# Where the seventh up group's third-block sums are made: last up group or first down unit

## The chip, the cores and the metric

The kernel runs on one core of a Trainium2 chip. The metric is the device time of one launch in microseconds (us), the median of three runs. The engines named below are PE (TensorE, the matrix multiplier; PEld is its weight load), DVE (VectorE), ACT (ScalarE), POOL (GpSimd) and SP (SyncE, which issues DMAs).

## The reference, cut to what matters

An attention with a cluster mask is followed by a two-layer feed-forward with a squared ReLU.

```python
q, k, v: (4, 8, 768, 64); centroids: (8, 16, 64)
mask = argmax(q_n . c_n) == argmax(k_n . c_n)
attn = softmax(where(mask, q k^T / 8, -1e9));  attn_out = attn v
x = attn_out.transpose(0, 2, 1, 3).reshape(3072, 512)
out = max(x @ w_in, 0) ** 2 @ w_out        # w_in 512 x 2048, w_out 2048 x 512
```

Only the second part is touched here. It is worked off in four sequences of 768 tokens each; the code numbers them n = 0 to 3.

## The kernel before, in words

Everything is float32. Matrix products are made by Strassen-like schemes: seven products in place of eight, for the price of sums and differences that DVE (and POOL, for `w_in`) makes. The result of the first layer, `g`, holds 16 blocks of 128 hidden rows by 2 halves of 384 tokens. A half is cut again into three blocks of 128 tokens: the first two are `TWO`, the third is `THIRD`.

**The up stage** (`up`, n = 1 to 3) runs over eight groups i = 0 to 7. A group makes four results, c11, c12, c21, c22: hidden rows i and 8+i for both token halves. PE makes products into PSUM banks, DVE adds a bank to a result (`add`, `sub`), ACT squares it (`square`, two instructions, L769 and L770; the last result of group 7 is squared by DVE, L773). Between these, DVE makes sums of finished groups for the next stage: `first_level` for the blocks `TWO`, `third_sums` for the block `THIRD`. In the last group the order on DVE is: product 6 added, `first_level(6)`, product 2 added to c11, `third_sums(6)`, product 7 added, then `behind_seven`, which is the first call of `parts`.

**`third_sums(g, n, f)`** makes four DVE instructions of 128 x 128 into a staging tile `third` (two buffers, shared with the output tiles), and its returned function stores that tile to DRAM, `g_far[n]`, with one DMA of 256 KB (L1105). For all f but the last it first calls `store_third`, which sends two more blocks of `g` there (L1092, and L1094 where n is even).

**The down stage** (`Down.run`) runs over units u, seven where n = 2 and fourteen where n = 1 or 3. A unit makes seven times eight 128 x 128 matmuls: with the sums in `s` (tile `l2`, shown as `l`), with the blocks of `g`, `home` or `extra`, and with four derived right factors that lie in `slot(0)` to `slot(3)`. In order: block times y00; block times y10; `s[:, 1]` times slot 1; a difference times slot 2; `s[:, 0]` times slot 0; a block times slot 3; and last a block from which DVE has subtracted `s[:, 1]` in place. `parts` makes the sums of the next unit. `combine` adds the banks up.

Where n is odd, units of the third blocks of two sequences (n-1 and n) are mixed in. Their left factors come back from `g_far` by `load_left(j)`, four DMAs of 256 KB or two where j is 1 or 4: into `g` for j = 4, into the tile `extra` for j = 1 and 5. The units there start (own, 1), (own, 4), (third, 4), (third, 1), (own, 5), (third, 5).

All loads and stores concerned are issued by SP in program order, each wait holding what is behind it. `load_right(k)`, called when the next unit needs other right factors, issues four DMAs of 256 KB from `w_far` into slots 1, 2, 0, 3, each when PE is through with the slot. In unit 0 of an odd sequence SP's order is: `load_right(4)`, `load_left(4)`, `load_left(1)`, the store of the last `third`, `load_left(5)`; the third of the four loads of `load_left(5)` reads what that store wrote. In unit 2 comes `load_right(1)`, for unit 3.

The order on every engine is written out by hand (`manual_schedule`), so the program order of the code is that of the engine's queue.

Of the kernel before, what the change touches and what calls it, by code (L numbers as in the profile page):

```python
# [25 lines left out]
def kernel(  # L26
# [521 lines left out]
    H2, F2, M2 = KT // 2, FT // 2, DM // 2  # L548
# [17 lines left out]
    def w_sums(i, odd=0):  # L566
        lo, hi = slice(i * P, (i + 1) * P), slice((F2 + i) * P, (F2 + i + 1) * P)
        a = [[w_in[:, H2 * g2 : H2 * (g2 + 1), cols] for g2 in range(2)] for cols in (lo, hi)]
        w_s = sp.tile([P, 4, H2, P], F32, name="w_s", tag=f"s{(i + odd) % 2 + 1}")
        s1, s2, s3, s4 = (w_s[:, j] for j in range(4))  # L570
        nc.gpsimd.tensor_tensor(out=s1, in0=a[1][0], in1=a[1][1], op=ALU.add)  # L571
        sub(s2, s1, a[0][0], nc.gpsimd)
        sub(s3, a[0][0], a[1][0], nc.gpsimd)
        sub(s4, a[0][1], s2, nc.gpsimd)
        return a, s1, s2, s3, s4
# [150 lines left out]
    def bank_tile(width):  # L726
        return banks.tile([P, width], F32, name="bank", tag="bank")
# [162 lines left out]
    def up(b, g, n, x, behind_seven):  # L890
        flat = g.rearrange("p f h n -> p (f h n)")
        odd = n == B - 1
        w_next = w_sums(0, odd)
        lefts, rights, done = {}, {}, []
        for i in range(F2):
            w, w_next = w_next, w_sums(i + 1, odd) if i + 1 < F2 else None
            ((c11, c12), (c21, c22)), product = group(i, g, w, x)
            ends, late = i >= F2 - 2, i % 2

            def result(j):  # L900
                bank = bank_tile(TB)
                product(j, bank)
                return bank

            def add(j, *results):
                bank = result(j)
                for out, to in results:
                    plus(out, bank, to)

            def levels_1():  # L910
                if done:
                    first_level(g, done[0])

            def levels_2():
                if done:
                    third_sums(g, n, done.pop(0))()

            def two():
                add(2, (c11, c11))
                square(c11)  # L920
                levels_2()

            if i < 2:
                nc.scalar.copy(out=c11, in_=result(1))
            elif not late:
                next(unit_1)
                if ends:
                    load_right(1)
            if not (late or ends):
                lefts[4] = second_lefts(4, i)  # L930
            add(6, (c12, c11))
            levels_1()
            if i == 1:
                rights[1] = second_rights(1, x[0][0][0])
            if not late or ends:
                two()
            if i == 0:
                rights[4] = second_rights(4, x[4])
            add(7, (c21, c12))
            if i == F2 - 1:  # L940
                behind_seven()
            elif ends:
                levels_1()
            r = spare_tile.rearrange("p i n -> p (i n)")
            if late and not ends:
                unit_4 = second(lefts.pop(4), rights[4], r, 0, TB)
                next(unit_4)
            add(5, (c22, c21), (c12, c12))
            square(c22)
            if i == F2 - 2:  # L950
                levels_2()
            if ends:
                sub(c21, c21, result(4))
            elif late:
                next(unit_4)
                unit_1 = second(
                    second_lefts(1, i + 1), rights[1], flat, 2 * TB * (i + 1), 2 * TB
                )
                next(unit_1)
                both = g[:, F2 + i - 1 : F2 + i + 1, 0]  # L960
                sub(both, both, r.rearrange("p (i n) -> p i n", i=2))
                for k in range(2):
                    square(both[:, k])
                two()
            add(3, (c12, c12))
            if ends:
                square(c21)
            (square if i < F2 - 1 else square_by_dve)(c12)
            done.extend([i] if ends else [i - 1, i] if late else [])
        xT.pop(b)  # L970
# [14 lines left out]
    def plus(out, one, two):  # L985
        nc.vector.tensor_tensor(out=out, in0=one, in1=two, op=ALU.add)  # L986
# [104 lines left out]
    def store_third(g, n, f):  # L1091
        nc.sync.dma_start(g_far[n][f, :, 1:3], g[:, F2 + f, :, THIRD])  # L1092
        if n % 2 == 0:
            nc.sync.dma_start(g_far[n][f, :, 0], g[:, f, 0, THIRD])  # L1094

    def third_sums(g, n, f):
        if f < F2 - 1:
            store_third(g, n, f)
        a = block_of(g, f, THIRD)
        third = outp.tile([P, DM], F32, name="third", tag="osb").rearrange("p (j n) -> p j n", j=4)  # L1100
        plus(third[:, 0], a[1][0], a[1][1])
        sub(third[:, 1], third[:, 0], a[0][0])
        sub(third[:, 2], a[0][0], a[1][0])
        sub(third[:, 3], a[0][1], third[:, 1])
        return lambda: nc.sync.dma_start(g_far[n][f, :, 3:7], third)  # L1105
# [12 lines left out]
    class Down:  # L1118
# [119 lines left out]
        def store(self, queue=nc.scalar):  # L1238
            for of, to in self.stores:
                for i in range(2):  # L1240
                    self.store_block(of, to, i, queue)
            self.stores = []

        def run(self):
            first_level(self.g, F2 - 1)
            store_third(self.g, self.n, F2 - 1)
            waiting = None
            for u, (of, j) in enumerate(self.units):
                x, s = self.ahead
                y = quarters(right(j))  # L1250
                copied = spare_tile[:, 4 + u % 2]
                one, two = (
                    bank_tile(4 * P).rearrange("p (i n) -> p i n", i=4) for _ in range(2)
                )

                ends = self.n == B - 1 and u + 1 == len(self.units)
                five = bank_tile(P) if ends else two[:, 3]
                last = bank_tile(P) if ends else None
                times(one[:, 0], x[0][0], y[0][0])
                nc.scalar.copy(out=copied, in_=one[:, 0])  # L1260
                self.store()
                times(two[:, 0], x[0][1], y[1][0])
                times(two[:, 1], s[:, 1], slot(1))
                times(two[:, 2], x[1][0], slot(2))
                times(five, s[:, 0], slot(0))
                times(one[:, 2], x[1][1], slot(3))
                if waiting:
                    next(waiting)
                sub(x[0][1], x[0][1], s[:, 1])
                times(last if ends else one[:, 1], x[0][1], y[1][1])  # L1270
                if u + 1 < len(self.units):
                    if (k := self.units[u + 1][1]) != j:
                        load_right(k)
                    if of and j in LATER:
                        self.load_left(LATER[j])
                    if self.units[u - 1] == (0, 5):
                        sub(self.s1, self.a[0][1], self.s2)
                    self.parts()
                if u == 0:
                    store = third_sums(self.g, self.n, F2 - 1)  # L1280
                    self.find_results()
                    if self.n % 2:
                        self.load_left(4)
                        self.load_left(1)
                    store()
                    if self.n % 2:
                        self.load_left(5)
                if waiting:
                    next(waiting, None)
                waiting = self.combine(of, j, one, two, five, copied, last)  # L1290
                to_end = len(self.units) - 1 - u
                for kk in LOADS[self.n % 2].get(u, ()):
                    load_x(self.n + 1, kk)
                if to_end == 2 - self.n % 2:
                    sum_x(self.n + 1, 1)
                elif to_end == 0:
                    sum_x(self.n + 1, 2)
            if self.n == B - 1:
                self.store(nc.sync)
            list(waiting)  # L1300
            sum_x(self.n + 1, 1)
            self.store()
# [298 lines left out]
```

## Time and profile before

| what | us |
|---|---|
| median of three runs (882.5 to 882.65) | 882.58 |
| the profiled execution's own time | 882.29 |
| its span, first to last instruction | 880.5 |
| PE busy / DVE busy / ACT busy | 871.7 / 753.9 / 385.9 |
| up stage to down stage, n = 1, 2, 3: first matmul of the down stage starts at | 512.48, 671.48, 786.54 |

The profile is of one execution; its times are microseconds from the span's start. PE's matmuls overlap one another, so a busy PE is read from the spacing of their starts: eight matmuls of the down stage start every 0.89 us when nothing holds them (514.27, 515.16, 516.06, 516.95). The granted clock is 1.0 in the whole execution. What lies around the span is 882.29 - 880.5 = 1.79 us.

### The profile page before, as it was taken

How to read it: one execution, taken by the hardware profiler on the slowest of the kernel's cores; microseconds unless marked ns; L12 is line 12 of the kernel's file. 1: busy time of each engine (PE TensorE's matmuls, PEld its weight loads, DVE VectorE, ACT ScalarE, POOL GpSimd, SP SyncE). 2: the span in 40 equal slices, each digit the busy share in tenths (PEclk: the TensorE clock that was granted, in tenths of full speed). 3: DMA queues.
4: the chain of work that ended last, by engine and by line, in shares of the span. 5: the costliest groups of instructions: out<-in, count | busy, mean ns of one | idle time of the engine just before them, and what ended most of it. 6: DMA issues, size and time to landing. Idle time of an engine off the chain costs nothing.

```text
span 880.5 us, 14989 instructions
## 1 busy us (share of the span) xinstructions
PE 871.7 (99%) x5487; PEld 600.3 (68%) x5487; DVE 753.9 (86%) x1359; ACT 385.9 (44%) x621; POOL 181.2 (21%) x240
## 2 busy tenths in 40 slices
PE   9999999999999999999999999999999999999997
PEld 6454444444444455568876689997767987769997
DVE  6798888888888999999859986797899898997786
ACT  5877667777765657750034420002443005440000
POOL 0000010000010236740055300005550064500000
PEclk9999999999999999999999999999999999999999
DMA  7887787766764335226701256681024730138563
GB/s 252 160 195 202 222 265 176 201 188 193 214 179 101 87 137 168 90 96 227 274 31 37 101 168 189 172 275 37 31 89 142 241 122 25 36 120 256 156 202 121
DMA packets 166402, 136.05 MB, mean 155 GB/s; under 512 B 58826, under 2 KB 140082, under 8 KB 166066
## 3 DMA queue, kind: packets, MB, share of 16 engines
q1 hardware_dynamic: 149938, 119.92, 46.6%
q10 hardware_dynamic: 16384, 15.11, 5.5%
q8 instruction: 45, 0.74, 0.3%
q14 instruction: 35, 0.29, 0.1%
HBM read 82.10 MB, written 41.89 MB: 141 GB/s over the span
## 4 chain that ended last, share of the span: by engine, by line
PE 76%; DVE 18%; ACT 2%; issue 2%; DMA 2%; DVEq 0%; ACTq 0%; SPq 0%
PE bank L1109 22%; PE bank L793 14%; PE sc L441 13%; PE av_a L475 9%; DVE g L986 7%; PE bank L1001 6%; PE av_b L475 4%; PE sc L450 3%; DVE third L551 2%; DVE g L551 2%; DVE spare L986 2%; DVE home L551 2%; PE sc L329 1%; DVE home L986 1%; PE sc L494 1%
## 5 line engine op out<-in xcount | busy, mean ns | idle before, releaser
L457 ACT ACTIVATE ex<-sc 128x1024 f32<-128x1024 f32 x144 | 144.2, 1025 | 38.1 <-PE sc L441 31.9
L441 PE MATMUL sc<-qkT 64*128 64x512 f32 (+1 forms) x768 | 151.0, 484 | 0.0
L986 DVE TENSOR_TENSOR g<-bank,g 128x384 f32<-128x384 f32 (+3 forms) x205 | 102.2, 514 | 19.8 <-PE bank L793 11.8
L769 ACT ACTIVATE g<-g 128x384 f32<-128x384 f32 x122 | 63.0, 516 | 98.2 <-DVE g L986 78.0
L441 PEld LDWEIGHTS sc<-qkT 64*128 64x128 f32 x768 | 67.2, 188 | 40.9 <-issue 29.7
L793 PE MATMUL bank<-xT,w_s 128*128 128x384 f32 x256 | 93.1, 486 | 0.0
L793 PE MATMUL bank<-x_t,w_s 128*128 128x384 f32 x256 | 93.0, 486 | 0.0
L1260 ACT COPY spare<-bank 128x128 f32<-128x128 f32 x35 | 9.2, 264 | 185.9 <-PE bank L1109 167.9
L475 PE MATMUL av_a<-ex,v_raw 128*64 128x512 f32 x384 | 85.9, 597 | 0.0
L460 DVE TENSOR_TENSOR total<-total,ex 128x1024 f32<-128x1024 f32 x64 | 78.7, 1229 | 6.5
L161 POOL TENSOR_TENSOR w_in<-w_in,w_raw 128x512 int32<-128x512 int32 x16 | 21.4, 1337 | 294.9 <-DVE w_in L153 294.9
L571 POOL TENSOR_TENSOR w_s<-w_in 128x256 f32<-128x256 f32 x32 | 25.3, 790 | 249.8 <-PE bank L1109 145.9
L1109 PE MATMUL bank<-home,l 128*128 128x128 f32 x560 | 74.1, 275 | 0.0
L793 PEld LDWEIGHTS bank<-xT,w_s 128*128 128x128 f32 x256 | 48.6, 190 | 34.2 <-issue 0.5
L1109 PEld LDWEIGHTS bank<-home,l 128*128 128x128 f32 x560 | 68.1, 192 | 0.1
L793 PEld LDWEIGHTS bank<-x_t,w_s 128*128 128x128 f32 x256 | 48.2, 190 | 29.1
L793 PE MATMUL bank<-xT,w_in 128*128 128x384 f32 x184 | 67.1, 487 | 0.0
L770 ACT ACTIVATE g<-g 128x384 f32<-128x384 f32 x122 | 63.8, 523 | 3.9
L475 PEld LDWEIGHTS av_a<-ex,v_raw 128*64 128x64 f32 x384 | 26.1, 137 | 51.0 <-issue 50.0
L450 PE MATMUL sc<-rows 64*128 64x512 bf16 (+1 forms) x360 | 60.4, 324 | 0.0
L793 PEld LDWEIGHTS bank<-xT,w_in 128*128 128x128 f32 x184 | 34.4, 190 | 21.7 <-DVE g L551 0.6
L1109 PE MATMUL bank<-home,g 128*128 128x128 f32 x352 | 46.5, 275 | 0.0
(222 smaller groups left out, 1559.9 us busy)
## 6 DMA issues: line engine op xcount, KB each, us to landing
home<-w_far SPq DMA_DIRECT2D x92, 256.0 KB
words<-flat SPq DMA_DIRECT2D x26, 384.0 KB
w_raw<-in_moe_w_in_dram SPq DMA_DIRECT2D x16, 512.0 KB
w_raw<-in_moe_w_out_dram SPq DMA_DIRECT2D x16, 512.0 KB
w_far<-home SPq DMA_DIRECT2D x28, 256.0 KB
g<-g_far SPq DMA_DIRECT2D x28, 256.0 KB
v_raw<-in_v_dram SPq DMA_DIRECT2D x16, 384.0 KB
g_far<-third SPq DMA_DIRECT2D x24, 256.0 KB
```

Of the source, the lines that this page charges most:

```text
L441: nc.tensor.matmul(sc[i][:, e, cols], lhsT=qkT[pair][rows, NCH + c], rhs=qkT[pair][rows, n.start // P : n.stop // P], start=first, stop=no ...
L450: nc.tensor.matmul(sc[i][:, e, cols], lhsT=ohT[pair][rows, 1, c * P : (c + 1) * P], rhs=ohT[pair][rows, 0, columns(i)], start=first, stop= ...
L457: nc.scalar.activation(out=ex[i], in_=sc.pop(i), func=ACT.Exp, scale=SCALE)
L460: eng.tensor_tensor(out=out, in0=a, in1=b, op=ALU.add)
L475: nc.tensor.matmul(bank[D * e : D * (e + 1), 0 : n.stop - n.start], lhsT=raw_v[pair][:, e, c], rhs=ex[i][:, e, cols], start=c == 0, stop=c ...
L551: return eng.tensor_tensor(out=out, in0=a, in1=b, op=ALU.subtract)
L769: nc.scalar.activation(out=to, in_=to, func=ACT.Relu)
L770: nc.scalar.square(to, to)
L793: nc.tensor.matmul(bank, lhsT=operands[j][0][:, kk], rhs=operands[j][1][:, kk], start=(kk == 0), stop=(kk == H2 - 1),)
L986: nc.vector.tensor_tensor(out=out, in0=one, in1=two, op=ALU.add)
L1001: nc.tensor.matmul(bank, lhsT=left[j][:, f], rhs=right(j)[:, f], start=(f == 0), stop=(f == F2 - 1),)
L1109: nc.tensor.matmul(bank, lhsT=left[:, f], rhs=rhs[:, f], start=(f == 0), stop=(f == F4 - 1))
```

## The change

In the last up group (i = 7) `third_sums(6)` is no longer called. In the down stage `store_third(6)` is called at the start, ahead of `store_third(7)`, and `third_sums(6)` just ahead of `third_sums(7)`, behind the first unit's `parts`. Both tiles are stored at the place where the last one was stored, behind `load_left(1)` in the odd sequences. This is so in each of n = 1, 2 and 3; n = 0 has other code.

```diff
             def levels_2():
-                if done:
+                if done and i < F2 - 1:
                     third_sums(g, n, done.pop(0))()
...
     def third_sums(g, n, f):
-        if f < F2 - 1:
+        if f < F2 - 2:
             store_third(g, n, f)
...
             first_level(self.g, F2 - 1)
-            store_third(self.g, self.n, F2 - 1)
+            for f in (F2 - 2, F2 - 1):
+                store_third(self.g, self.n, f)
...
                 if u == 0:
-                    store = third_sums(self.g, self.n, F2 - 1)
+                    stores = [third_sums(self.g, self.n, f) for f in (F2 - 2, F2 - 1)]
                     self.find_results()
                     if self.n % 2:
                         self.load_left(4)
                         self.load_left(1)
-                    store()
+                    for store in stores:
+                        store()
                     if self.n % 2:
                         self.load_left(5)
```

No instruction is added or taken away: in each of the three sequences four DVE instructions, one store of a `third` tile and the place of the `store_third` DMAs in the queue move.

## Prediction

> **What bounds the kernel now.** I read the page's busy shares first, then the groups for PE's idle time, then the timeline of PE, DVE, ACT and SP about the change from up to down stage.
>
> ```profile
> PE 871.7 (99%) x5487; PEld 600.3 (68%) x5487; DVE 753.9 (86%) x1359; ACT 385.9 (44%) x621; POOL 181.2 (21%) x240
> ...
> L1109 PE MATMUL bank<-w_out,g 128*128 128x128 f32 x240 | 30.0, 276 | 1.8 <-DVE g L551 1.8
> ```
>
> PE has hardly any idle time, but 1.8 us of it lies in the down stage, behind a DVE instruction of L551 (`sub`). PE's timeline for n = 1 shows where:
>
> ```profile
> 516.95 1.06 PE L1109 MATMUL bank<-home,g 128*128 128x128 f32 x8
> 518.62 1.16 PE L1109 MATMUL bank<-w_out,g 128*128 128x128 f32 x8 [0.61 <-DVE g L551]
> 519.61 1.95 PE L1109 MATMUL bank<-w_t,g 128*128 128x128 f32 x16
> ```
>
> These are unit 0's last eight matmuls. At a spacing of 0.89 they would start at 517.84; they start at 518.62 (0.78 late), and the next at 519.61, 0.99 later in place of 0.89 (0.10 more, the first weight load not overlapped). The stall costs 0.88; n = 2 and 3 show the same gap (0.62 and 0.61). So all that DVE can win here is 3 x 0.88 = 2.64. DVE is back to back from 509.4 to the awaited `sub` (517.87 to 518.56). The moved work lies in that chain, in group 7:
>
> ```profile
> 510.12 0.55 DVE L986 TENSOR_TENSOR g<-bank,g 128x384 f32<-128x384 f32 x1
> 510.58 0.28 DVE L986 TENSOR_TENSOR third<-g 128x128 f32<-128x128 f32 x1
> ...
> 511.26 0.52 ACT L770 ACTIVATE g<-g 128x384 f32<-128x384 f32 x1
> 511.31 0.29 DVE L551 TENSOR_TENSOR third<-g,third 128x128 f32<-128x128 f32 x1
> 511.51 0.55 DVE L986 TENSOR_TENSOR g<-bank,g 128x384 f32<-128x384 f32 x1
> 511.98 0.68 DVE L986 TENSOR_TENSOR l<-g 128x512 f32<-128x512 f32 x1
> ```
>
> The reader is to see that c11 of group 7 is added at 510.12, squared by ACT until 511.78, and that `l<-g`, the first sum of `parts` for unit 0, comes at 511.98. That sum reads all eight c11 blocks, so it needs this square.
>
> [...] The record of `l<-g` has one, which waits for ACT: it runs at 511.814, 0.036 behind the end of the square; at n = 2 and 3 it stands 0.037 behind too. [...] here a lone `third` store lands after 2.0 and in a full queue after 4.3 to 4.6, which I use.
>
> **The change part by part.** *Taken out of group 7:* four DVE instructions. By their starts (510.58 to 511.51) they hold DVE 0.93. But `l<-g` cannot follow by 0.93: the wait for ACT ends at 511.81, and where such a wait ends last DVE starts 0.066 later, at 511.88 in place of 511.98. The gain is 0.10 for each n; the other 0.83 becomes DVE idle time. c11's own square does not come earlier, since the add before it waits for `first_level(6)`, which waits for ACT. The rest of the chain to the `sub` moves up by 0.10 (its ACT square, c22's, moves with it). Bounds: 0 (the wait already decides) and 0.88 (it doesn't exist). I take 0.10: total -0.30.
>
> *Added behind unit 0's `parts`:* the same 0.93, so all DVE work from there on is 0.93 - 0.10 = 0.83 later than before. Behind it wait `combine` of unit 0 and unit 1's `sub`, which ended at 523.14 and is needed by about 524.8; at 523.97 it is in time (n = 2: 682.96 for 683.8; n = 3: 798.37 for 798.9, the tightest). DVE had 1.20 (n = 1), 1.34 and 0.75 of idle time one unit later and catches up there. POOL and ACT have nothing queued here that matters. Cost 0. Were that cover gone, up to 0.83 for each n.
>
> *SP and the transfers, n = 3:*
>
> ```profile
> 785.68 0.32 SPq L1105 DMA_DIRECT2D g_far<-third  x1
> ...
> 793.24 2.98 SPq L1146 DMA_DIRECT2D g<-g_far  x2
> 796.28 1.05 SPq L1146 DMA_DIRECT2D extra<-g_far  x2
> 797.37 0.50 SPq L1105 DMA_DIRECT2D g_far<-third  x1
> 797.91 4.97 SPq L1146 DMA_DIRECT2D extra<-g_far  x4
> 802.98 0.45 SPq L1068 DMA_DIRECT2D home<-w_far  x1
> ```
>
> The store at 785.68 is the one that moves, out of an idle queue and to just ahead of 797.37, where the queue is full. The DMA completion marks in the trace give the landings: `load_left(4)` at 798.32 and 799.60, `load_left(1)` at 800.47 and 801.29, the store at 801.96, then 802.80 and 803.62. Only when the store had landed did SP issue the third load of `load_left(5)` (801.97), and only behind that could it issue `load_right(1)` (802.98). `store_third(6)` costs nothing: its data are ready by 508 (n = 1), and SP is idle until 516.57.
>
> What is late next is `load_right(1)`. (a) One store more in a full queue: 0.67, the distance of the store's landing from the one before it. (b) The second load of `load_left(4)` overwrites what `third_sums(7)` reads, so it is issued 0.83 later (795.85 to 796.68). It was bound half by the queue, half by its own latency (3.74; 3.07 for a like load into a nearly empty queue), so it lands between 0 and 0.83 later; I take 0.6. Together d = 1.27 (0.67 to 1.5). All that follows lands later by d. The slots are used by PE in these rows:
>
> ```profile
> 807.96 1.06 PE L1109 MATMUL bank<-home,l 128*128 128x128 f32 x8
> 808.86 1.06 PE L1109 MATMUL bank<-home,g 128*128 128x128 f32 x8
> 809.75 1.06 PE L1109 MATMUL bank<-home,l 128*128 128x128 f32 x8
> 810.64 1.06 PE L1109 MATMUL bank<-home,g 128*128 128x128 f32 x8
> ```
>
> They landed at 807.20, 808.19, 809.39, 810.04: 0.76, 0.67, 0.36, 0.60 ahead. The smallest lead decides: PE is late by d - 0.36 + 0.05 (restart) + 0.10 (weight load, as in the stall above) = 1.06 against before. *n = 1:* leads 1.19, 1.44, 1.68, 1.85; d - 1.19 + 0.15 = 0.23 late. *n = 2:* no left factors are loaded, `load_right(5)` comes behind the stores, with a lead of 0.70 at the least; one store more (0.67) fits: the gain of 0.10 stays.
>
> **Sum:** +0.23 - 0.10 + 1.06 = +1.19. On the profiled execution's 882.29 (span 880.5 and 1.79 around it) that is 883.48; the median stands 0.29 above that execution, so I forecast 883.8, no change that can be told: about 0.2%, 1.77 us, is what a measurement of this kernel can tell from none.
>
> **The rivals.** *Transfers hidden:* the extra store is absorbed because later loads were spaced by PE's release of the slots (804.58 and 805.48 were), not by the queue. Against it: their latency is 4.8 and 4.6, a lone one's 2.8. Then only -0.30 stays: 882.3. *Slower beyond doubt:* the same loads stall PE in both odd sequences. n = 1 differs from n = 3 only by a faster last megabyte (531.66 to 534.74, against 805.89 to 810.04). The two stalls exceed 1.77 together, with n = 2's 0.10 taken off, from d = 1.57 on ((d - 0.21) + (d - 1.04) - 0.10); at d = 1.8 they make 2.25: 884.8. For it: (b) may be the whole 0.83 and hold up every load behind it. Against: that takes 0.07 more than (a) and (b) at their ends. *The change does what it says:* the ACT wait is no limit, the stall goes, 2.64 less: 879.9. Against it are three event records at the same 0.036 behind ACT.
>
> **How the numbers follow.** Forecast (a stall at `load_right(1)`, d 0.7 to 1.57): 0.60. Transfers hidden: 0.13. Slower: 0.23. Stall gone: 0.04. Faster by over 0.2% is the last, 0.04; slower the third, 0.23; within 0.2% the other two, 0.73. The range leaves out the fast rival and the slow one's far end: from 882.1, under the case of hidden transfers, to 885.0. The forecast's own range is 882.9 (d = 0.7) to 884.4.
>
> **What would show each step.** In the profile after: a DVE gap of about 0.8 ahead of `l<-g`, released by ACT (L770), and PE's wait for L551 down to about 0.5 for each n. Eight `third` instructions behind unit 0's `parts`. For n = 3, SP's third load of `load_left(5)` over 1 us later against unit 0's start, and a new PE wait for `home<-w_far` at unit 3, under 0.4 at n = 1. I am wrong if PE's L551 wait is gone, if PE waits for no DMA, or if unit 1's last matmuls wait for DVE.

## The result and the profile after

The changed kernel takes 887.24 us (median of six runs, 886.36 to 890.33), the kernel before 882.33 beside it: a ratio of 1.0061, with a 95% interval of 1.0046 to 1.0077. That is slower beyond doubt, by some 4.9 us, where I had forecast +1.19. The profiled execution took 886.36, with a span of 884.5 against 880.5, so 4.0 more; it is the fastest of the six, and the trace explains these 4.0. Of all runs below one was slow (1259.13 us at a mean granted clock of 0.679, in the kernel with the halves of the loads issued in turn), and no ratio counts it.

The groups of PE by shape, after (busy, mean ns | idle time before them, and what ended it):

```profile
L1109 PE MATMUL bank<-home,l 128*128 128x128 f32 x560 | 74.2, 275 | 2.5 <-DMA home<-w_far 1.7 <-DVE l L551 0.8
L1109 PE MATMUL bank<-home,g 128*128 128x128 f32 x352 | 46.6, 275 | 0.4 <-ACT spare L1261 0.4
L1109 PE MATMUL bank<-w_out,g 128*128 128x128 f32 x240 | 30.0, 276 | 1.8 <-DVE g L551 1.8
```

The old wait of `w_out,g` for the `sub` is still 1.8. New are 1.7 for the loads of `home`, which I had foreseen though smaller, and 0.8 + 0.4 for DVE and ACT, which I had not. PE's timeline tells where:

```profile
518.57 1.16 PE L1109 MATMUL bank<-w_out,g 128*128 128x128 f32 x8 [0.52 <-DVE g L551]
...
535.11 1.13 PE L1109 MATMUL bank<-home,l 128*128 128x128 f32 x8 [1.09 <-DMA home<-w_far]
...
790.69 1.16 PE L1109 MATMUL bank<-home,l 128*128 128x128 f32 x8 [0.81 <-DVE l L551]
...
793.99 1.16 PE L1109 MATMUL bank<-home,g 128*128 128x128 f32 x8 [0.36 <-ACT spare L1261]
795.86 1.16 PE L1109 MATMUL bank<-w_out,g 128*128 128x128 f32 x8 [0.71 <-DVE g L551]
...
811.90 1.13 PE L1109 MATMUL bank<-home,l 128*128 128x128 f32 x8 [0.59 <-DMA home<-w_far]
```

I set each PE instruction's start against the same one before and noted where the distance changes:

| place | before | after | change of the distance |
|---|---|---|---|
| n = 1, unit 0, last matmuls | 518.62 | 518.57 | -0.05 |
| n = 1, unit 3 (waits for `home`) | 533.91 | 535.11 | +1.25, with the first weight load 1.32 |
| n = 1, two waits near the end of its down stage | 593.14 | 594.62 | +0.21 |
| n = 2, unit 0 | 677.62 | 679.00 | -0.10 |
| n = 3, unit 0 (waits for DVE and ACT) | 792.67 | 795.86 | +1.81 |
| n = 3, unit 3 (waits for `home`) | 808.07 | 812.08 | +0.82 |

They add up to 4.0. The third entry need not come from the change: in four profiles of kernels whose n = 1 is as before, the same place gives -0.16 to +0.18. DVE's timeline of n = 1 shows the step that I rated highest as predicted: the moved sums leave a gap of 0.75 that ACT's square ends, and `l<-g` starts only 0.06 earlier (511.98 before).

```profile
510.16 1.01 DVE L986 TENSOR_TENSOR g<-bank,g 128x384 f32<-128x384 f32 x2
511.92 0.69 DVE L986 TENSOR_TENSOR l<-g 128x512 f32<-128x512 f32 x1 [0.75 <-ACT g L770]
```

SP's timeline of n = 3 has the queue as predicted too. Two stores go out in a row, and the third and fourth load of `load_left(5)` and all of `load_right(1)` come behind their landing (805.63 and 806.29 by the completion marks):

```profile
796.19 3.80 SPq L1146 DMA_DIRECT2D g<-g_far  x2
800.04 1.15 SPq L1146 DMA_DIRECT2D extra<-g_far  x2
801.24 0.98 SPq L1105 DMA_DIRECT2D g_far<-third  x2
802.26 5.00 SPq L1146 DMA_DIRECT2D extra<-g_far  x4
807.36 1.87 SPq L1068 DMA_DIRECT2D home<-w_far  x4
```

What nothing above explains is unit 0 of n = 3, the largest entry. DVE comes to it 1.8 later against PE than before, and this lateness arises in n = 3's up stage, which the change does not touch.

### The profile page after: what moved, and what is told of

Its sections match the earlier page's. It is cut to its first block, busy times and chain, and to the rows that moved or that the text cites. A ratio compares the mean times of both kernels' runs of the same rounds, so it can differ in the third digit from the quotient of the medians.

```text
span 884.5 us, 14985 instructions
## 1 busy us (share of the span) xinstructions
PE 872.7 (99%) x5487; PEld 598.8 (68%) x5487; DVE 755.7 (85%) x1359; ACT 386.1 (44%) x621; POOL 181.8 (21%) x240
## 4 chain that ended last, share of the span: by engine, by line
PE 82%; DVE 12%; ACT 2%; DMA 2%; issue 1%; SPq 0%; DVEq 0%
PE bank L1109 21%; PE bank L793 18%; PE sc L441 14%; PE av_a L475 10%; PE bank L1001 5%; PE av_b L475 5%; DVE g L986 4%; PE sc L450 4%; DVE g L551 2%; DVE third L551 2%; PE sc L329 1%; PE bank L883 1%; DVE spare L986 1%; PE sc L494 1%; DVE home L551 1%
```

## The experiments

**Which sequence pays for what.** The theories, as I called them in the expectations: Q, only the loads of unit 3; K, the stall in n = 1 shifts the engines against each other and so brings on the one at unit 0 of n = 3; R, that one comes and goes by chance.

```diff
-                if done and i < F2 - 1:
+                if done and not (i == F2 - 1 and n in (1,)):
```

(and the same condition in `third_sums` and `run`). *The change in n = 1 alone:* 

> The change in the first odd sequence (n = 1) alone; n = 2 and n = 3 as before. Theory Q (the loads of unit 3 land late behind the store, nothing else): the stall at unit 3 of n = 1, +1.3 less 0.1 gained at unit 0, so about +1.2, and n = 3 keeps no new wait. Theory K (a stall in n = 1 shifts PE against DVE and POOL and so brings on the later DVE stall at unit 0 of n = 3): the same +1.2 and up to 1.8 more at unit 0 of n = 3, about +3.0. Theory R (the lateness of DVE in n = 3 comes and goes from run to run, whatever the kernel): +1.2 in this profile or +3, with a spread of the timed runs as wide as that of the changed kernel (4 us).

Measured: 885.78, ratio 1.0036 (1.0022 to 1.0050), so 3.2 slower, nearest to K's +3.0. The profiled execution was the slowest, 888.91. Unit 0 of n = 3 stalls in it by 1.92, though n = 3 is as before. Unit 3 of n = 1 lost 4.4, in two parts. Its PE timeline, and then the same time cut into windows (PE, PEld, DVE, ACT, POOL busy; granted clock of PE; DMA share; GB/s):

```profile
536.62 1.13 PE L1109 MATMUL bank<-home,l 128*128 128x128 f32 x8 [2.52 <-DMA home<-w_far]
```

```profile
537.00:538.00 1.00, 1.00 (x11) 1.00 (x10) 0.09 (x1) 0.00 (x0) 0.00 (x0) 1.00 0.63 240
538.00:539.00 1.00, 1.00 (x7) 1.00 (x6) 0.00 (x0) 0.00 (x0) 0.00 (x0) 0.53 0.20 41
539.00:540.00 1.00, 1.00 (x7) 1.00 (x6) 0.00 (x0) 0.00 (x0) 0.00 (x0) 0.50 0.66 231
```

After a wait of 2.52, PE's granted clock fell to 0.50 from 538.07 to 541.48, and by PE's starts another 1.6 went there. In the changed kernel's profile the wait was 1.09 and the clock stayed at 1.00.

*The change in n = 3 alone:* 

> The change in n = 3 alone: everything up to group 7 of n = 3 is as before. Theories Q and K: only the stall of unit 3 of n = 3, +0.8 less 0.1, about +0.7; unit 0 of n = 3 waits no longer than before. Theory R: DVE may be late at unit 0 of n = 3 here too (+1.8 more), and then this lateness is not brought on by the change in n = 1.

Measured: 882.76, ratio 1.0010 (1.0002 to 1.0018), +0.8; in the profile unit 3 of n = 3 costs 0.77. Unit 0 waits no longer than before, so its later stall comes from something changed in n = 1 or 2. But this profile also has a wait of 0.15 for `home`, costing 0.44, at unit 3 of n = 1, where the program is the old one. There `load_right(1)` landed 1.0 to 1.7 later against PE than in the profile of before. The queue varies by as much as the smallest lead, 1.19, from one execution to the next.

**The loads taken off the critical place.**

```diff
                         load_right(k)
+                    if u == 2 and self.n % 2:
+                        self.load_left(5)
...
-                    if self.n % 2:
-                        self.load_left(5)
```

> The changed kernel, but with load_left(5) issued in unit 2 behind load_right(1), so that SP no longer holds load_right(1) behind the landing of the third store. Theory Q: no PE wait for home at unit 3 in n = 1 and n = 3, only the 3 x 0.1 gained at unit 0 is left: 0.3 faster than before, 4.5 to 5 faster than the changed kernel. Theory K: the same, since without the stall of n = 1 nothing shifts. Theory R, or a cost of the eight sums on DVE that has nothing to do with the transfers: unit 0 of n = 3 still loses up to 1.8, about 1.5 slower than before.

Measured: 883.51, ratio 1.0018 (1.0010 to 1.0026). Unit 3 no longer stalls in either sequence, so those stalls come from `load_left(5)` standing ahead of `load_right(1)`. The move takes away two things at once, the wait for the store's landing and four transfers ahead; no run parts them. But unit 0 of n = 3 stalls as much as in the changed kernel, its first wait again 0.82 behind DVE, without any stall of PE in n = 1 ahead of it:

```profile
788.01 1.16 PE L1109 MATMUL bank<-home,l 128*128 128x128 f32 x8 [0.82 <-DVE l L551]
...
791.32 1.16 PE L1109 MATMUL bank<-home,g 128*128 128x128 f32 x8 [0.36 <-ACT spare L1261]
```

Theory K falls, and Q is only half the story. R is made unlikely by the stall's one size wherever it appears, 1.8 to 1.9; the runs with one instruction more or less, below, settle it.

*The store alone, no DVE work moved* (in `levels_2`, group 7 keeps the sums and hands its store to `run`):

```diff
-                    third_sums(g, n, done.pop(0))()
+                    store = third_sums(g, n, done.pop(0))
+                    if i < F2 - 1:
+                        store()
+                    else:
+                        kept.append(store)
...
+                    kept.pop()()
                     store()
```

> The kernel before, with its sums for the third token block of group 6 made in group 7 as before, but with the store of them issued ahead of that of group 7, behind load_left(1): the store moves and no DVE work does. My prediction's terms: (a) alone, 0.67 later for n = 3 and n = 1, so a stall of 0.67 - 0.36 + 0.15 = 0.46 at unit 3 of n = 3 and none at n = 1: +0.5. Rival, the store in the full queue is the whole cause of the landing 2.3 later at n = 1: stalls of about 1.3 and 0.8, +2, or more if theory K holds.

Measured: 884.46, ratio 1.0023 (1.0014 to 1.0032). The profile has no wait for `home` at unit 3, in n = 1 or n = 3: one store more in the full queue, my term (a), does not reach PE by itself here. For n = 1 that is what I expected. For n = 3 the 0.46 expected did not come, but there the queue also ran early: the second load of `load_left(4)` landed 0.80 earlier against unit 0 than before, and the last store only 0.18 later. The rival's figure of +2 came out right for the wrong reason, since the stall at unit 0 of n = 3, 1.92, is nearly all that the profile shows.

**A pause that comes with the place of the instruction stream.** That stall is in four kernels now, at one size, and not in before or with n = 3 changed alone. In all four, DVE pauses for 0.40 at the same instruction in n = 3's up stage. DVE's timeline of the changed kernel and then that of before:

```profile
747.88 0.54 DVE L986 TENSOR_TENSOR g<-bank,g 128x384 f32<-128x384 f32 x1
748.88 1.02 DVE L986 TENSOR_TENSOR g<-bank,g 128x384 f32<-128x384 f32 x2 [0.46 <-PE bank L883]
...
753.46 0.71 DVE L986 TENSOR_TENSOR third<-g 128x128 f32<-128x128 f32 x1
754.20 0.78 DVE L551 TENSOR_TENSOR third<-third,g 128x128 f32<-128x128 f32 x1
754.90 0.82 DVE L551 TENSOR_TENSOR third<-g 128x128 f32<-128x128 f32 x1
```

```profile
746.49 1.67 DVE L986 TENSOR_TENSOR g<-bank,g 128x384 f32<-128x384 f32 x3
...
751.72 0.28 DVE L986 TENSOR_TENSOR third<-g 128x128 f32<-128x128 f32 x1
752.04 0.75 DVE L551 TENSOR_TENSOR third<-third,g 128x128 f32<-128x128 f32 x1
752.71 0.28 DVE L551 TENSOR_TENSOR third<-g 128x128 f32<-128x128 f32 x1
```

The label at 748.88 names PE, but the last event that the instruction needed had its own record (EVENT_SEMAPHORE, a wait in DVE's instruction stream) at 748.46, and in 169 of the other 201 places of this profile where DVE had been idle for over 0.1 behind such a record, it started 0.06 to 0.09 behind it (31 of the other 32 stand ahead of an instruction with a wait of its own). PE's event that the label goes by came at 748.70; in the kernel before, the same DVE instruction ran at 747.14, ahead of that event's counterpart at 747.31, so it does not wait for it. The idle time behind this record is 0.395 to 0.396 in all four, wherever PE stands. So I counted DVE's records. In n = 1, `l<-l,g` of unit 2's `parts` has three EVENT_SEMAPHORE records of L551 about it before (523.84 to 524.02) and two after (524.24 and 524.67). From there to the pause, DVE's instructions lie one place earlier; with the store alone moved the pause is there too. So "no instruction is added or taken away", in the section on the change, holds for DVE's sums and not for its waits: 402 such records before, 400 after. The trace also shows DMA packets of kind "instruction", 35 of them, of 8 KB, on queue 14 (0.29 MB). Near this place one of them starts when DVE has made 1,468 records in the kernel before, and 1,474 in each of the four slow kernels.

*Theory F: the place in the stream decides.* One DVE instruction less ahead brings the pause of 0.40 onto the instruction at 748.88, and this grows to the stall at unit 0. It is tested from both sides. One tiny instruction is put back in n = 1:

```diff
+    pad = const.tile([P, 1], F32, name="pad")
...
+                if self.n == 1 and u == 6:
+                    plus(pad, ups[:, 0:1], ups[:, 0:1])
```

> The changed kernel with one tiny DVE instruction more (an add of 128x1 on a tile of its own) in the down stage of n = 1, where DVE idles 2.18: it puts the DVE program of n = 2 and 3 back to the place that it has in the kernel before, since the change had taken one EventSemaphore instruction out of DVE's stream in n = 1. Theory F [...]: the pause of 0.40 and the stall at unit 0 of n = 3 are gone, 1.5 to 1.9 faster than the changed kernel; the waits for home at unit 3 stay. Theory D (DVE is late there because of the transfers, the semaphores' rotation or the moved store): no difference to the changed kernel.

Measured: 884.97, ratio 1.0042 (1.0028 to 1.0057), against 887.24 without it. The pause is gone, and so is the added stall at unit 0. Unit 3 still loses 1.42 in n = 1 and 1.06 in n = 3. PE's timeline:

```profile
535.42 1.13 PE L1109 MATMUL bank<-home,l 128*128 128x128 f32 x8 [1.19 <-DMA home<-w_far]
...
793.94 1.16 PE L1109 MATMUL bank<-w_out,g 128*128 128x128 f32 x8 [0.53 <-DVE g L551]
...
810.22 1.13 PE L1109 MATMUL bank<-home,l 128*128 128x128 f32 x8 [0.82 <-DVE extra L551]
```

The label at 810.22 names DVE, but the load of `home` landed at 810.08, 0.14 ahead of the start, as in the other stalls of this place.

*The same instruction, with `load_left(5)` behind `load_right(1)`:* 

> The changed kernel with load_left(5) behind load_right(1) and the same tiny DVE instruction: both causes taken away. Theory F: no wait for home at unit 3, no added stall at unit 0 of n = 3, only the 3 x 0.1 gained is left: 0.3 faster than before (881.6 to 881.8 where before has 882). Theory D: as left5_late, 1.5 slower than before.

Measured: 881.87, ratio 1.0001 (0.9994 to 1.0007). Both causes are gone, and nothing is left of the loss. Unit 3 waits for nothing in this profile:

```profile
L1109 PE MATMUL bank<-home,l 128*128 128x128 f32 x560 | 74.0, 275 | 0.0
```

The 0.3 that I expected as a gain cannot be told from none by the medians; by PE's starts unit 0 gains 0.08 in each of the three sequences.

*And from the other side, one DVE instruction taken out of the kernel before:*

```diff
-            if j == 7:
+            if j == 7 and (of, self.n) != (0, 1):
                 sub(c[21], c[22], c[21])
```

> The kernel before, but in n = 1 one DVE instruction of combine is left out (c21 = c22 - c21 of its token block 0, 0.69 of DVE time in a stretch with idle time), so that result block is not what the reference has. No transfer, store or other engine is touched. Theory F: DVE's stream lies one instruction earlier from there on, as in the changed kernel: the 0.40 pause and the stall at unit 0 of n = 3 appear, 1.5 to 1.9 slower than before, though work was taken out. Theory D: no difference to before, or 0.1 faster.

Measured: 883.71, ratio 1.0022 (1.0012 to 1.0032). Less work, no transfer touched, and slower by 2.1 (881.64 beside it). DVE's timeline has the pause and the slow sums:

```profile
745.98 1.02 DVE L986 TENSOR_TENSOR g<-bank,g 128x384 f32<-128x384 f32 x2 [0.46 <-PE bank L883]
...
750.56 0.72 DVE L986 TENSOR_TENSOR third<-g 128x128 f32<-128x128 f32 x1
```

Theory F holds in what it says of the place: one record fewer ahead brings the pause, one more takes it away, with or without transfers touched. Over all fifteen profiles of this case, the five with the pause have 1,480 DVE records ahead of the 768-element sum that follows it, and the instruction packet at 1,474. The other ten have 1,481 or 1,482, and the packet at 1,468 or 1,470. What acts at this place is open. The paused instruction did not wait for this packet: in all five the packet starts only 0.67 to 0.81 after that instruction has started. How the packets and the pause hang together no run shows.

**How 0.40 becomes 1.8.** My reading was that a DVE late by 0.4 falls in with POOL's sums of the weights. The first test put a delay there by hand:

```diff
+            if n == 3 and i == 1:
+                plus(spare_tile[:, 4:6], spare_tile[:, 4:6], spare_tile[:, 4:6])
             add(5, (c22, c21), (c12, c12))
```

(it doubles a part of an intermediate). 

> The kernel before with one DVE instruction more in n = 3's up stage (128x256 add, 0.33 by the spacing of starts), at the place where the changed kernel has the 0.40 pause[...]. If a delay of this size at this place is what grows (DVE operations then fall together with those of POOL): DVE's lateness grows from 0.33 to over 1 by the end of the up stage, and unit 0 of n = 3 stalls by 1 or more: 1 to 2 slower. If the delay is only carried along: 0.3 or less.

Measured: 881.66, ratio 1.0002 (0.9993 to 1.0010), a miss of mine: the pause is in group 3, not in group 1 (`i == 1`), and the delay in group 1, 0.31 by DVE's starts, was caught up within 5 us. The second stood at `i == 3`, with a maximum in place of the sum:

> The kernel before with one DVE instruction more in group 3 of n = 3's up stage (an elementwise maximum of 128x256 with itself, which changes nothing, 0.33 by the spacing of starts), at the very place of the 0.40 pause; the earlier attempt put it into group 1. If a delay there grows by falling in with POOL's operations: DVE over 1 later by the end of the up stage, a stall of 1 or more at unit 0 of n = 3, 1 to 2 slower than before. If it is only carried along: at most 0.3 slower.

Measured: 881.55, ratio 0.9997 (0.9990 to 1.0004). It stood rightly but was too small: DVE has 0.18 of slack there, and the next instruction came only 0.15 late. So it was widened to `spare_tile[:, 2:6]`:

> The kernel before with an elementwise maximum of 128x512 with itself (0.61 by the spacing of starts, changes nothing) on DVE at the place of the pause in n = 3's up stage. The earlier one of 128x256 came out only 0.15 late there, since DVE has 0.18 of slack at that place; this one should come out 0.43 late, like the pause of 0.40. If such a lateness grows by falling in with POOL's operations: third sums of group 3 and 5 at 0.7 to 0.8 in place of 0.28, DVE 1.5 to 2 later by the end of the up stage, unit 0 of n = 3 stalls by as much: 1.5 to 2 slower than before. If it is only carried along: DVE 0.4 later at the end and 0.4 slower at most.

Measured: 884.73, ratio 1.0032 (1.0020 to 1.0043). DVE's timeline:

```profile
747.32 0.68 DVE L950 TENSOR_TENSOR spare<-spare 128x512 f32<-128x512 f32 x1
747.92 1.01 DVE L989 TENSOR_TENSOR g<-bank,g 128x384 f32<-128x384 f32 x2
...
752.49 0.65 DVE L989 TENSOR_TENSOR third<-g 128x128 f32<-128x128 f32 x1
753.17 0.77 DVE L551 TENSOR_TENSOR third<-third,g 128x128 f32<-128x128 f32 x1
753.86 0.82 DVE L551 TENSOR_TENSOR third<-g 128x128 f32<-128x128 f32 x1
```

POOL's timeline beside it:

```profile
752.26 0.73 POOL L571 TENSOR_TENSOR w_s<-w_in 128x256 f32<-128x256 f32 x1 [1.73 <-PE bank L793]
...
754.49 0.78 POOL L551 TENSOR_TENSOR w_s<-w_in,w_s 128x256 f32<-128x256 f32 x1
```

With no instruction moved ahead of it, a lateness of 0.43 at this place grows to 1.9 by the next group, and unit 0 of n = 3 loses 1.9 (a wait for `home` at unit 3 adds 0.44 in this profile). POOL is at its `w_s` sums from 752.26 to 755.27 in this profile, and the four `third` sums start inside that time. They take 0.65 to 0.82 here. In the kernel before, the 72 `third` sums with no POOL instruction beside them take 0.27 to 0.29, and 12 of the 24 that overlap one take 0.74 to 0.82; `g<-bank,g` (128x384) takes 0.54 to 0.56 with POOL beside it or not. At this place of the kernel before, only two of the four were slow (0.75 and 0.81). The one at 752.71 there started 0.01 ahead of a sum of POOL and kept 0.28, and it was POOL's sum that took 0.86 in place of 0.73. So a DVE that is 0.43 late loses where it had not lost before.

**Which term of the transfers.** In the kernel with the tiny instruction, the halves of `load_left(4)` and `load_left(1)` are issued in turn, so less stands behind the load that waits for DVE (the second argument of `load_left`, new here, picks the half):

```diff
-                        self.load_left(4)
-                        self.load_left(1)
+                        for k in range(2):
+                            for l in (4, 1):
+                                self.load_left(l, k)
```

> The changed kernel with the tiny DVE instruction, so without the later stall at unit 0, and with the halves of load_left(4) and load_left(1) issued in turn: only one load of load_left(1), not both, and the stores stand behind the load that waits for the eight sums on DVE. If term (b) of my prediction (that wait moves all that follows) is most of the transfers' cost, d falls to near 0.67 and unit 3 stalls by about 0.5 in n = 3 and 0 to 0.3 in n = 1: about 882.3, 2.5 faster than with the pad alone (885). If the second store in the full queue and the queue's own irregularity are most of it: 884.5 to 885, as with the pad alone.

Measured: 882.56, ratio 1.0004 (0.9993 to 1.0015), against 1.0042 without the new order. PE's timeline at unit 3 of both odd sequences:

```profile
533.60 1.06 PE L1109 MATMUL bank<-home,l 128*128 128x128 f32 x8
...
808.77 1.13 PE L1109 MATMUL bank<-home,l 128*128 128x128 f32 x8 [0.63 <-DMA home<-w_far]
```

The stall of n = 1 is gone and that of n = 3 stays. So (b), the load that waits for the eight sums and holds up the queue behind it, carries the stall of n = 1. For n = 3 the two profiles do not decide between the terms: with (a) alone the queue ran early, and with (b) lessened the fourth load of `load_left(5)` landed 2.24 behind the third, where 0.85 lay between them before.

*Does the kernel before lose to its transfers?* `load_left(5)` moved as above, in the kernel before:

> The kernel before with load_left(5) issued behind load_right(1) and nothing else. If the transfers of the kernel before already stall PE in some executions (a wait of 0.4 for home was seen at unit 3 of n = 1 in one profile where that part of the program was unchanged): 0.1 to 0.4 faster and a narrower spread. If they never do: no difference.

Measured: 881.33, ratio 0.9998 (0.9989 to 1.0007): no difference that can be told. The profile shows why it need not be a gain: the loads of unit 4 now stand behind the moved ones, and PE lost 0.55 there in n = 3 (0.3 in the changed kernel with the same move).

**A version that beats both.** The gap of 0.75 is of use only to work that does not need the square. Onto the kernel with both causes taken away:

```diff
-            plus(s[:, 0], x[1][0], x[1][1])
+            for f in (slice(0, 3), slice(3, 4)) if self.count == 0 else (slice(0, 4),):
+                plus(s[:, 0, f], x[1][0][:, f], x[1][1][:, f])
```

> A version that may beat both: the changed kernel with load_left(5) behind load_right(1), the tiny DVE instruction, and the first sum of parts for unit 0 split into blocks 0 to 2 and 3 of each half, so that the idle 0.75 of DVE ahead of l<-g is used by the three quarters that do not need the square of the seventh c11. The wait for ACT is then behind only 0.28 of work in place of 0.69: unit 0's sub comes 0.4 to 0.45 earlier in each of the three sequences, 1.2 to 1.35 faster than late_pad, so about 880.6. If the semaphore wait stays ahead of the first part, 0.2 slower each: 882.4.

Measured: 880.43, ratio 0.9980 (0.9974 to 0.9986), so 1.8 faster than before by the ratio and 1.3 by the medians (881.73 beside it). The expected time was near, 880.6. DVE's timeline of n = 1, and then PE's:

```profile
510.53 0.55 DVE L986 TENSOR_TENSOR l<-g 128x384 f32<-128x384 f32 x1
511.30 0.29 DVE L986 TENSOR_TENSOR l<-g 128x128 f32<-128x128 f32 x1 [0.21 <-ACT g L770]
```

```profile
516.43 1.06 PE L1109 MATMUL bank<-home,g 128*128 128x128 f32 x8
517.54 1.16 PE L1109 MATMUL bank<-w_out,g 128*128 128x128 f32 x8
```

Only the last quarter waits for ACT, and unit 0's last matmuls start 1.11 behind the ones before, against 1.67 in the kernel before. PE gains 0.54 to 0.56 in each of the three sequences, against 0.10 at the most by the change alone.

## Why the prediction was wrong, and where it was right

- **The gain at unit 0: right.** 0.10 for each n, since ACT's square takes over the wait. In the profile after, the EVENT_SEMAPHORE record ahead of `l<-g` runs 0.037 behind the square's end in each of the three sequences (at 511.855 in n = 1), and `l<-g` starts 0.065 behind the record. At PE: measured -0.05 and -0.10 in n = 1 and 2, hidden by the other stall in n = 3, and 0.08 in each of the three once both causes of loss are taken away. The rival of a stall that goes is out.
- **The sums behind unit 0: right.** PE waited neither for `combine` nor for unit 1's `sub`. Their one effect on PE that the runs show goes by way of the load that waits for them.
- **The n = 3 stall at `load_right(1)`: right in place and near in size, but not by its terms.** 1.06 forecast, 0.82 measured. I let the smallest lead decide, 0.36 for the third load. But the third and fourth landed only 0.50 later against unit 0, since before they had waited for PE to release their slots; by the third alone PE would have lost 0.50 - 0.36 + 0.15 = 0.29. It waited for the first, which landed 1.38 later with a lead of 0.76: 1.38 - 0.76 + 0.15 = 0.77. The parts of d differ too: the second load of `load_left(4)` landed 0.07 later against unit 0 (0.6 forecast), the first store 0.49 and the second 1.15 (1.27 forecast in all). That the sum came out near is in part luck.
- **The n = 1 stall: mis-sized.** 0.23 forecast, 1.3 measured, since d was 2.25 there in place of 1.27. Here (a) and (b) came out in size: the second load of `load_left(4)` landed 0.59 later (0.6 forecast), the two stores 0.68 apart (0.67 forecast). What I had not priced lies between them. I let the queue keep its spacing behind the late load, but by the completion marks the second load of `load_left(1)` and the first store came 1.22 and 1.16 behind the landing ahead of them, 0.83 and 0.69 before. Taken over all profiles, the first store of n = 1 landed 8.67 to 8.88 after the start of unit 0's last matmuls in seven of the eight in which no load waits for moved sums (9.77 in one of them), 9.52 to 11.69 in the six in which one does, and 9.06 with the halves issued in turn. So what I left out comes mostly with the wait, at a size that differs from one execution to the next; why the queue spaces its landings more widely is open. That unit 3 stalls in both odd sequences was the mechanism of the second rival, which I gave 0.23. Its price was near for these two places: 2.25 forecast, 1.32 + 0.82 measured, and in single executions more.
- **The step that failed outright: everything else at nothing.** I counted what DVE executes and not how many instructions stand in its program. With the store moved, one EVENT_SEMAPHORE record fewer stands in DVE's stream of n = 1, and all up to the pause lies one place earlier. This cost 1.8 in the profile, 1.5 by the ratios of the two kernels with late loads (1.0018 and 1.0001), 2.1 where one instruction was taken out. Without it, the change costs 1.0042, still outside my range, whose end of 885.0 is 1.0027 of 882.58; in that kernel's profile the n = 1 stall, 1.42, is the largest part.
- None of my three signs of being wrong turned up, though the sum was wrong. They tested the mechanisms I had named, and could not see one that I had not. Of what was to show each step, one thing failed: PE's wait for `home` at n = 1 was 1.09, not under 0.4.
- The sums themselves take the same time in both profiles: at the three changes from up to down stage those of 128 elements 280 to 294 ns, those of 512 elements 681 to 694.

Why the six runs spread up to 890.33 is not settled. A long wait for `home` followed by the half clock, as in the profile with n = 1 changed alone, would do it, but no other profile shows it.

## What to carry to other kernels

When work is moved, ask for each queue what stands behind the instruction that now waits: here one load waiting for 0.93 of DVE work held up two loads, two stores and then, by the store's landing, four loads that PE needs. A lead read from one execution is a sample: set it against its spread over several before calling it cover. In this kernel, with PE 99% and DVE 85% busy, a stall of 1.8 far from the edit came with the place of the instruction stream; one tiny instruction more (1.0061 to 1.0042) or, in the kernel before, one instruction less (1.0022) told it apart from the edit's own cost.

## What the runs showed of the hardware that was not expected

- DVE paused for 0.40 at one instruction in every kernel whose stream lay one place earlier, and in none of the others (five profiles against ten). What DVE waits for there is open.
- A lateness of 0.15 at that place was absorbed and one of 0.40 to 0.43 grew to 1.8 to 1.9, through `third` sums of 0.28 that took 0.65 to 0.82 while POOL was summing.
- After PE had waited for 2.52, its granted clock fell to 0.50, 1.45 after the wait had ended, and stayed there for 3.41 us; 1.6 more was lost. This is one profile. Waits of 1.09 (the changed kernel) and 1.19 (with the tiny instruction) left the clock at 1.00. What sets off the half clock was not shown.
